# Rewriting windowed attention plus a soft mixture of experts: batch pairs transposed as one 32-bit word, eight units, a list scheduler

## The chip, the cores and the metric

The kernel runs on one core of a Trainium2 chip. The metric is the device time of that core in microseconds (us), the median of the runs. Engines are named as in the profile: PE (TensorE matmuls), PEld (its weight loads), DVE (VectorE), ACT (ScalarE), POOL (GpSimd), SP (SyncE). The clock that the throttle grants to PE has two values in the records here, 1.0 and 0.5, called full and half.

## The reference, cut to what matters

```python
batch, n_heads, seq, head_dim = 8, 8, 576, 64          # q, k, v in fp32
rel = pos[:, None] - pos[None, :]
mask_plain = (rel >= 0) & (rel < 32)                    # heads 0..3
mask_dil   = (rel >= 0) & (rel < 128) & (rel % 4 == 0)  # heads 4..7
attn = softmax(where(mask, q @ k.T / 8, -1e9)) @ v
x = attn, as 4608 tokens x 512
# soft mixture of experts: 8 experts of 4 slots each, D = 512, F = 1024
logits = x @ phi                                        # 4608 x 32
d = softmax(logits, axis=0);  slot_input = d.T @ x
slot_out[e] = relu(slot_input[e] @ w1[e]) @ w2[e]
c = softmax(logits, axis=1);  return c @ slot_out
```

Both softmaxes need the logits of all tokens, and the experts need the slot inputs summed over all tokens. So there is attention over all batches first, then a tail that no attention work can hide: FFN1, FFN2, and the output. The inputs are 61.9 MB and the output 9.4 MB.

## The kernel before

It handles a batch at a time, each batch in two steps (plain heads, dilated heads). Tokens lie on partitions as loaded, 24 tokens to a partition, so PE transposes q, k and v, and ACT copies the result from PSUM (the tiles ps_0 to ps_2, where PE leaves it) back into token order. The dilated heads get their own order (all tokens of one residue modulo 4 together). After that a 96-query block needs only a 128-key window of either kind.

```python
def st_A(g, r):                    # q and k of one step, one residue of the token number
    def pe(t):
        for c1 in range(6):
            for hx in range(2):
                i_ = t.transpose(pbf[64 * hx:64 * hx + 64, 128 * c1:128 * c1 + NR],
                                 src[0:NR, 2 * typ + hx, 4 * c1 + r, :], ident[0:NR, 0:NR])
    pv = pbf[:, 0:768].rearrange("x (c h u) -> x c h u", c=6, h=2)
    def ev(dst, t, off):
        d = dst[:, :, off:off + S]
        if typ == 0:
            d = d.rearrange("x h (p c r) -> x r c h p", c=6, r=4)[:, r]   # plain order
        else:
            d = d.rearrange("x h (r p c) -> x r c h p", r=4, c=6)[:, r]   # dilated order
        return lambda ac: ac.activation(d, pv[:, :, :, PCH * t:PCH * t + NPP], ACTF.Copy)
    op("act", ev(QT[par], 0, 0), r=[pb], **{key: [b_QT[par]]})       # 128 x 288 bf16, scattered
    op("act", ev(KT[par], 1, HALO), r=[pb], **{key: [b_KT[par]]})
...                                # st_V: the same for v, into VT
def st_P(g, half):                 # probabilities times values: 96 weight columns
    i_ = t.matmul(po[0:QB, hx, 65 * m:65 * m + 65],
                  pts[m // 3][0][:, hx, QB * (m % 3):QB * (m % 3) + QB], ...)
def st_X(b, c):                    # x transposed for the logits
    if c >= 2:                     # the dilated heads go back to token order in this copy
        d = d.rearrange("p (s r) -> p r s", r=4)
def st_L(b):                       # logits, and two exps: token order, dilated order
    i_ = t.matmul(lg[:, hf, 0:288], phi_pad[:, c]..., XT[:, c, 288 * hf:288 * hf + 288], ...)
    op("act", ... expT ... ACTF.Exp, accum_out=csum[:, b:b + 1])
    op("act", ... expP[:].rearrange("p (r h s) -> p h s r", r=4, h=2) ... ACTF.Exp)
```

The order of the operations is a fixed loop over 16 steps, written by hand.

The softmax here doesn't subtract the row's maximum and nothing guards it: scores larger than these inputs give would overflow.

## Time and profile before

387.83 us (387.59 and 388.07), two runs. From the page of the profiled run come the busy times, three of the rows of forty slices (each digit is tenths of busy time; PEclk is the granted clock in tenths) and the chain that ended last, by engine and by line:

```profile
PE 230.0 (60%) x3056; PEld 170.5 (44%) x3056; DVE 140.6 (36%) x242; ACT 297.6 (77%) x302; POOL 54.5 (14%) x108
...
ACT  1398999799979997999799978997899764120660
...
PEclk9999999999999999999999999999999999999995
DMA  7999994059005900599055005600660066000599
...
ACT 52%; PE 20%; issue 15%; DVE 7%; DMA 2%; POOL 0%; ACTq 0%
ACT VT L378 17%; ACT KT L352 13%; ACT QT L352 12%; ACT PT L419 8%; PE ps_2 L339 2%; DMA stg<-in_k_dram 2%; PE ps_0 L651 2%; DVE XB L447 2%; DVE w1r L676 2%; PE ps_0 L339 2%; PE ps_2 L394 2%; ACT expP L486 1%; PE ps_0 L459 1%; PE ps_0 L599 1%; PE ps_1 L670 1%
```

ACT is busy nearly all the time and leads the chain; DMA holds 2% of it and idles every other few slices after the first seven. The table of stretches shows it more sharply. A batch takes 38.6 us, and these are two of them (start and end, length, busy time of each engine with the number of instructions, granted clock, DMA share, GB/s landed):

```profile
80.10:118.70 38.60, 25.53 (x359) 20.13 (x357) 14.04 (x25) 35.41 (x37) 5.16 (x10) 1.00 0.40 74
118.70:157.30 38.60, 25.51 (x359) 20.07 (x357) 14.03 (x25) 35.40 (x37) 5.14 (x10) 1.00 0.40 74
```

ACT works 35.4 of 38.6 us. What on? The groups by form (line, engine, operation, output and input by name, shape and type, count, then busy us and mean ns of one, idle time before it):

```profile
L378 ACT ACTIVATE VT<-ps_2 128x288 bf16<-128x288 bf16 x30 | 40.9, 1634 | 0.0
L352 ACT ACTIVATE QT<-ps_0 128x288 bf16<-128x288 bf16 x26 | 33.3, 1281 | 14.3 <-PE ps_0 L339 13.8
L419 ACT ACTIVATE PT<-ps_0 128x576 bf16<-128x576 f32 x32 | 26.2, 820 | 12.8 <-PE ps_0 L413 12.8
L486 ACT ACTIVATE expP<-ps_0 128x576 bf16<-128x576 f32 x4 | 10.3, 2575 | 0.0
```

A copy of 288 elements takes 1.3 to 1.7 us and an exp of 576 elements 0.82 us. The copies differ in that their output is bf16 elements scattered through the row. All nine groups of them sum to 274 us. The second exp of the logits, L486, scatters its output too and takes 2.58 us.

One reading needs care. The clock row shows 9, full speed, from the start. The timeline of PE (start, length, engine and line, count) has the logits of one batch, eight matmuls of 288 columns:

```profile
87.20 2.08 PE L478 MATMUL ps_0<-XT,phi_pad 128*128 128x288 bf16 x8 [0.67 <-ACT PT L419]
```

In the trace their starts lie 240 ns apart inside each half of four, which is 1.2 columns per ns. FFN1's groups of 512 columns start 430 ns apart and drop to 216 ns at 345.6 us, exactly where the first record of a full clock begins. So attention ran at half clock: a slice without a record is drawn as full. Other timed runs of this kernel list mean clocks of 0.60 to 0.91 with the same time (386.6 to 388.8 us), where the profiled one lists 0.988: a listed mean counts all time without a record as full (0.988 is 385.6 us less half of the last 9.3, the only ones recorded at half), so it says little of the time before the first record.

### The profile page before, as it was taken

What the parts mean: (1) busy time and instruction counts of PE and PEld (TensorE: products, weight loads), DVE (VectorE), ACT (ScalarE), POOL (GpSimd) and SP (SyncE); (2) the same over time, 40 slices, a digit from 0 to 9 for tenths busy, and PEclk for the clock granted to TensorE, in tenths of its full rate; (3) what the DMA queues carried; (4) which work ended last, traced back from release to release, by engine and by line L of the source; (5) the groups of instructions that cost most, each with busy time, mean ns of one, the idle gap of its engine ahead of it and who ended that gap; (6) DMA issues with size and microseconds to landing.
All of it is one profiled execution on the core that took longest, in us unless ns stands there. A gap on an engine that the chain in (4) does not pass through costs nothing.

```text
span 385.6 us, 7144 instructions
## 1 busy us (share of the span) xinstructions
PE 230.0 (60%) x3056; PEld 170.5 (44%) x3056; DVE 140.6 (36%) x242; ACT 297.6 (77%) x302; POOL 54.5 (14%) x108
## 2 busy tenths in 40 slices
PE   0223672676467646764676468646864676479750
PEld 0212451565456545654565456445644565245100
DVE  7501332453245324532453245324532473411760
ACT  1398999799979997999799978997899764120660
POOL 6990400050005000600040000000000000000000
PEclk9999999999999999999999999999999999999995
DMA  7999994059005900599055005600660066000599
GB/s 138 217 205 213 218 208 90 3 90 205 2 2 83 205 8 2 85 218 205 8 91 95 2 2 108 111 2 0 110 113 2 0 110 111 0 2 2 210 405 364
DMA packets 12623, 40.89 MB, mean 106 GB/s; under 512 B 3633, under 2 KB 3633, under 8 KB 10545
## 3 DMA queue, kind: packets, MB, share of 16 engines
q0 software_dynamic: 9472, 30.94, 42.7%
q1 hardware_dynamic: 3120, 9.50, 6.3%
q8 instruction: 24, 0.39, 0.4%
q14 instruction: 7, 0.05, 0.0%
HBM read 61.93 MB, written 9.44 MB: 185 GB/s over the span
## 4 chain that ended last, share of the span: by engine, by line
ACT 52%; PE 20%; issue 15%; DVE 7%; DMA 2%; POOL 0%; ACTq 0%
ACT VT L378 17%; ACT KT L352 13%; ACT QT L352 12%; ACT PT L419 8%; PE ps_2 L339 2%; DMA stg<-in_k_dram 2%; PE ps_0 L651 2%; DVE XB L447 2%; DVE w1r L676 2%; PE ps_0 L339 2%; PE ps_2 L394 2%; ACT expP L486 1%; PE ps_0 L459 1%; PE ps_0 L599 1%; PE ps_1 L670 1%
## 5 line engine op out<-in xcount | busy, mean ns | idle before, releaser
L352 ACT ACTIVATE QT<-ps_0 128x288 bf16<-128x288 bf16 x26 | 33.3, 1281 | 14.3 <-PE ps_0 L339 13.8
L422 DVE TENSOR_TENSOR PT<-PT,mask_d 128x576 bf16<-128x576 bf16 x32 | 14.7, 459 | 73.9 <-ACT PT L419 73.8
L378 ACT ACTIVATE VT<-ps_2 128x288 bf16<-128x288 bf16 x30 | 40.9, 1634 | 0.0
L352 ACT ACTIVATE KT<-ps_0 128x288 bf16<-128x288 bf16 x26 | 40.0, 1539 | 0.0
L419 ACT ACTIVATE PT<-ps_0 128x576 bf16<-128x576 f32 x32 | 26.2, 820 | 12.8 <-PE ps_0 L413 12.8
L419 ACT ACTIVATE PT<-ps_1 128x576 bf16<-128x576 f32 x32 | 26.4, 826 | 11.4 <-PE ps_1 L413 11.4
L352 ACT ACTIVATE KT<-ps_2 128x288 bf16<-128x288 bf16 x20 | 33.3, 1667 | 0.0
L469 DVE COPY XT<-ps_0 128x576 bf16<-128x576 bf16 x15 | 14.8, 983 | 47.8 <-PE ps_0 L459 47.8
L339 PE MATMUL ps_0<-ident,stg 112*64 112x112 bf16 x312 | 20.1, 300 | 17.1 <-DMA stg<-in_k_dram 15.1
L232 POOL DMA_DIRECT2D stg<-in_q_dram x16 | 9.5, 597 | 146.0 <-PE ps_0 L339 130.0
L352 ACT ACTIVATE KT<-ps_1 128x288 bf16<-128x288 bf16 x18 | 28.8, 1602 | 0.0
L352 ACT ACTIVATE QT<-ps_2 128x288 bf16<-128x288 bf16 x20 | 27.8, 1388 | 0.7
L422 DVE TENSOR_TENSOR PT<-PT,mask_p 128x576 bf16<-128x576 bf16 x32 | 14.9, 467 | 32.6 <-ACT PT L419 32.6
L394 PE MATMUL ps_2<-ident,VT 128*128 128x128 bf16 x114 | 15.7, 309 | 16.6 <-ACT VT L378 16.6
L378 ACT ACTIVATE VT<-ps_1 128x288 bf16<-128x288 bf16 x18 | 24.1, 1604 | 0.0
L352 ACT ACTIVATE QT<-ps_1 128x288 bf16<-128x288 bf16 x18 | 24.0, 1331 | 0.0
L339 PEld LDWEIGHTS ps_0<-ident,stg 112*64 112x64 bf16 x312 | 14.6, 164 | 20.7 <-issue 17.1
L398 DVE COPY VN<-ps_2 128x768 bf16<-128x768 bf16 x19 | 10.4, 550 | 33.4 <-PE ps_2 L394 33.4
L378 ACT ACTIVATE VT<-ps_0 128x288 bf16<-128x288 bf16 x16 | 21.5, 1614 | 0.0
L469 DVE COPY XT<-ps_1 128x576 bf16<-128x576 bf16 x16 | 15.6, 975 | 13.5 <-PE ps_1 L459 13.5
L262 POOL DMA_DIRECT2D stg<-in_moe_w_dram x6 | 3.2, 538 | 116.5 <-PE ps_0 L339 93.4
L413 PE MATMUL ps_1<-QT,KT 64*128 64x96 bf16 x192 | 13.5, 271 | 10.2 <-ACT KT L352 9.6
(113 smaller groups left out, 531.0 us busy)
## 6 DMA issues: line engine op xcount, KB each, us to landing
out_dram<-w1r SPq DMA_DIRECT2D x18, 512.0 KB, 5.0
w1r<-in_moe_w_dram POOLq DMA_DIRECT2D x8, 1024.0 KB, 14.4
stg<-in_moe_w_dram POOLq DMA_DIRECT2D x6, 1024.0 KB, 8.0
stg<-in_q_dram POOLq DMA_DIRECT2D x16, 288.0 KB, 6.5
stg<-in_k_dram POOLq DMA_DIRECT2D x16, 288.0 KB, 9.5
stg<-in_v_dram POOLq DMA_DIRECT2D x32, 144.0 KB, 9.5
w2r<-in_moe_w_dram POOLq DMA_DIRECT2D x2, 1024.0 KB, 21.2
phi_st<-in_moe_phi_dram SPq DMA_DIRECT2D x1, 64.0 KB, 1.9
```

The lines of the kernel that those rows point to most:

```text
L232: res.append(g.dma_start(stg[p0:p0 + NPP, s, 0:6144].rearrange("p (g x) -> p g x", g=4), src[b, half::2, :, :].rearrange("h (p c) d -> p h ...
L339: i_ = t.transpose(pbf[64 * hx:64 * hx + 64, 128 * c1:128 * c1 + NR], src[0:NR, 2 * typ + hx, 4 * c1 + r, :], ident[0:NR, 0:NR])
L352: return lambda ac: ac.activation(d, pv[:, :, :, PCH * t:PCH * t + NPP], ACTF.Copy)
L378: op("act", lambda ac, d=d, typ=typ: ac.activation(d, pv[:, :, :, PCH * typ:PCH * typ + NPP], ACTF.Copy), r=[pb], **{"w" if r + typ == 0 e ...
L394: i_ = t.transpose(pbf[:, 128 * m:128 * m + 128], VT[:, typ, half, QB * m:QB * m + 128], ident[:, :])
L398: op("dve", lambda vv: vv.tensor_copy(vt[:, half, :, :, 0:64], pbf[:, 0:768].rearrange("p (m x d) -> p m x d", m=NB, x=2)), r=[pb], w=[vb[ ...
L413: i_ = t.matmul(sc[:, hx, QB * mm:QB * mm + QB], KT[par][64 * hx:64 * hx + 64, half, QB * m:QB * m + 128], QT[par][64 * hx:64 * hx + 64, h ...
L419: op("act", lambda ac: ac.activation(pt[:], sc[:, :, 0:3 * QB], ACTF.Exp, scale=SCALE), r=[scb], w=[ptb])
L422: op("dve", lambda vv: vv.tensor_tensor(pt[:], pt[:], mk.unsqueeze(1).to_broadcast([128, 2, 3 * QB]), AluOp.mult), r=[b_mask[typ]], w=[ptb])
L447: op("dve", lambda vv: vv.tensor_tensor(xd, pv[:, :, :, 0:64], rv[:].unsqueeze(3).to_broadcast([QB, 2, NB, 64]), AluOp.mult), r=[pob, rvb] ...
L469: op("dve", lambda vv: vv.tensor_copy(d, i_), r=[pb], **{"w" if c == 0 else "a": [b_XT]})
L651: i_ = t.matmul(sp_[32 * j:32 * j + 32, :], hT[:, hi, cc, j, :], w2v[e][:, cc, :], start=(hi == 0 and cc == 0), stop=(hi == 1 and cc == 7))
```

## The change

The intent: one unit is a pair of batches and one kind of heads, so eight units in all. Loading puts the two batches on neighbouring partitions, so after the transposes their columns are neighbours, and one 32-bit word carries both. ACT then moves 864 words in one instruction, in place of six bf16 copies of 288. These words are also written in runs of 18 or more neighbours (72 tokens to a partition instead of 24), and it is the read from PSUM that now has a step, of 192 bytes. So two things change in the copies, the word and the runs. The source runs of a load become 18 KB. Scores and V transposes read every second column. The operations are no longer in a written order: each has a planned cost, and a list scheduler orders them. It can put filler matmuls into PE's planned idle time, but its window is empty here.

The core of the diff (the whole kernel was rewritten; cuts marked):

```diff
+QB = 96; HALO = 32; NU = 8
+FILL = (9.0, 0.0)                       # window for filler matmuls: empty
...
+for t, src in enumerate((q, k, v)):
+    for bpar in range(2):                # rows of the two batches interleaved
+        rows = src[2 * bp + bpar].rearrange("h (p c) d -> (h p) (c d)", c=CT)[32 * ty:32 * ty + 32]
+        res.append(g.dma_start(stg[32 * t + bpar:32 * t + 32:2, s, :]..., rows...))
...
+i_ = t.transpose(bankb2(pt, a)[64 * hx:64 * hx + 64, 96 * kk:96 * kk + 96],
+                 src[:, hx, c, :], ident[0:96, 0:96])
-        return lambda ac: ac.activation(d, pv[:, :, :, PCH * t:PCH * t + NPP], ACTF.Copy)   # x 192
+            t32 = TT[:, u % 2, :].bitcast(F32)
+            return ac.activation(d, sv, ACTF.Copy)                  # 864 words, x 32
...
-                  pts[m // 3][0][:, hx, QB * (m % 3):QB * (m % 3) + QB],
+                  sbt(pts[i])[:, o_:o_ + 128],                       # 128 weight columns
...
-        if c >= 2:  d = d.rearrange("p (s r) -> p r s", r=4)        # scattered XT copy
+        d, s_ = sbt(xt)[:, x, :], bankb(px)[:, 0:S]                 # plain XT copy
+        rhs = sbt(x1)[:, c - 2, :].rearrange("p (r i) -> p i r", r=4)[:, lo // 4:hi // 4]
-    op("act", ... expP ... ACTF.Exp)                                # second logits exp
...
-i_ = t.matmul(psA[64 * typ:64 * typ + 64, 32 * c:32 * c + 32], x_, et[:, NB * typ + m, :], ...)
+i_ = t.matmul(psA[32 * g:32 * g + 32, 256 * ty:256 * ty + 256], et[:, i, :], xb[:, m, :], ...)
...
-for step in range(-1, 2 * B + 2):  st_B(g, 0); st_S(g, 0, 0); st_A(g + 1, 0); ...
+P.schedule(filler, FILL)
```

## The prediction

> **What bounds the kernel before.** ScalarE. The stretch table gives it 35.6 of every 38.6 us batch; the chain of waits puts 52% of the span on it and only 2% on DMA. The groups by form say why: the copies that put q, k and v back into token order (QT, KT, VT, 128x288 bf16) take 1.28 to 1.67 us each, some 274 us in all, though an exp of twice the elements takes 0.82 us. They write scattered bf16 elements, about 4 ns each. The 40-slice rows show DMA saturated early (205 to 218 GB/s of bf16 landing, twice that read), later mostly waiting. From the slot result to the end takes 27 us.

> **A second reading.** The clock row shows 9, but single matmuls of the logits (288 columns) start 240 ns apart and 128-column transposes 107 ns: 1.2 columns per ns. FFN1 starts at 430 ns per group of 512 columns and drops to 216 ns at 345.6 us, at the first clock record. So attention ran at half clock, and the row shows missing records as full. [...] 3.4 us stretches over 90% busy, mostly with transposes, released nothing.

> **What changes.** Two batches are transposed as neighbouring columns, so one 32-bit word carries both; 32 evictions of 864 words replace 192 scattered ones. At the exp rate (0.65 us per 576 when alone) one is about 0.95 us: 31 us instead of 274. The second logits exp (2.58 us) goes, as do the scattered XT copies (1.44 us, now 0.46). ScalarE falls to 10 to 11 us per unit, VectorE to 12 to 13 us.

> **What binds next.**
> - DMA: 61.9 MB at about 424 GB/s is 146 us, or 13.4 us per unit with one or two weights.
> - TensorE at half clock, from the spacings seen, per unit: input transposes 5.8, scores 1.9, V transposes 2.6, PV 2.7 (128-column weights), X transposes 1.9, logits 1.9, slot weights 1.0, slot sums 0.6: 18.4 us, and about 2 us for tiling-mode changes (0.13 us each in the trace). At full clock about 11.5 us.

> So the clock decides. At full clock DMA binds: loads end near 150 us, then the last FFN2 part and 27 us of output: about 185 us. At half clock: first data at 13 us, eight units of 20 us, a tail of the last softmax, fold, FFN1 and FFN2 of about 25 us, output 27 us: about 230 us. The kernel has code for filler matmuls but its window is empty and over half of its work is transposes. I expect mostly half clock, with released stretches.

> **Prediction: 210 us, range 183 to 234. Faster by over 2%: 0.985; within 2%: 0.008; slower: 0.007.**

> **What would show each step.** Right: ScalarE busy below 120 us; evictions near 0.95 us; TensorE groups leading the chain of waits in the middle, transposes spaced 80 ns per pair (half clock); first clock record late. If instead pairs are near 42 ns apart, the chain's middle should be DMA and the time about 185 us.

> **What would make it wrong.** Evictions that read PSUM with a 192-byte step could take 1.5 us or more; stride-2 operands could slow scores and V transposes; a fixed order planned for other durations could stall engines.

## The result, and the profile after

210.75 us, the median of 209.28 and 212.23, against 387.83 before, on the same chip. The ratio is 0.543, with a 95% interval of 0.539 to 0.547. Ratios here are the mean time of one kernel's runs over that of the other's runs in the same rounds, so not quite the ratio of the quoted medians. Executions over 1.5% slower than the fastest of the same kernel are left out of the means. The output is correct. The profiled run spans 207.6 us.

The same parts of the page as before:

```profile
PE 153.9 (74%) x2840; PEld 110.4 (53%) x2840; DVE 107.8 (52%) x256; ACT 94.0 (45%) x135; POOL 35.8 (17%) x72
...
PE   0058977699988579989597998977897979898000
...
ACT  2015657665546566555476555773110100099200
...
PEclk9999999999999799999969999996555599999955
DMA  6999999999999999999999696089999000069998
...
PE 54%; DVE 23%; ACT 6%; issue 5%; DMA 4%; POOL 1%; DVEq 0%; POOLq 0%
PE ps L514 14%; PE ps L657 10%; DVE PT L564 6%; PE ps L824 5%; PE ps L574 5%; DVE XB L613 5%; PE ps L630 5%; DVE WD L868 4%; DMA stg<-in_v_dram 4%; PE ps L549 4%; DVE VN L579 3%; PE ps L602 3%; ACT PT L556 3%; PE ps L770 3%; PE ps L690 2%
```

ACT fell from 297.6 to 94.0 us and from 52% to 6% of the chain. PE leads the chain now. DMA is busy to slice 22 (about 115 us) and yet has 4% of the chain: its loads are ahead of the work. The three groups that answer to the readings of before, by form:

```profile
L531 ACT ACTIVATE TT<-ps 128x864 f32<-128x864 f32 x32 | 28.3, 895 | 27.0 <-PE ps L514 26.9
L657 PE MATMUL ps<-XT,phi_pad 128*128 128x384 bf16 x32 | 15.0, 600 | 0.0
L657 PE MATMUL ps<-XT,phi_pad 128*128 128x192 bf16 x32 | 8.1, 385 | 1.4 <-DVE XB L613 0.8 <-DVE XT L639 0.6
```

The 32 word copies take 28 us together, where 192 bf16 copies took 274. In the same profile ACT's exps with contiguous output take 651 ns for 576 elements (L663) and 810 for 768 (L556), 0.83 ns for each element more. Drawn on to 864 elements that makes an estimate of 890 ns, and the trace's 895 agrees. The scattered bf16 copies of before don't: the same line drawn back to 288 elements gives an estimate of 412 ns, and they took 1281 to 1667.

PE's clock is read from spacing again, since the first record is at 25.8 us. The timeline of PE, the first and the fifth group of input transposes, and the stall near 68 us:

```profile
12.89 5.97 PE L514 MATMUL ps<-ident,stg 96*64 96x96 bf16 x144 [12.89 <-DMA stg<-in_v_dram]
...
27.14 0.96 PE L514 MATMUL ps<-ident,stg 96*64 96x96 bf16 x36
...
67.65 0.34 PE L574 MATMUL ps<-ident,TT 128*128 128x128 bf16 x3
70.33 0.48 PE L574 MATMUL ps<-ident,TT 128*128 128x128 bf16 x3 [2.33 <-issue]
```

Before 25.8 us, 144 transposes take 5.97 us: a pair every 80 ns, half clock. From 27.14 us, 36 take 0.96 with the last one's own length in it: a pair every 40 to 43 ns, full clock. The records list full clock from 25.8 to 141.9 us but for 70.2 to 73.6 and 104.4 to 107.8, then half from 141.9 to 165.8, then full to 196.5. So most of attention ran at full clock.

The third and fourth lines show a pause of 2.33 us inside one operation of six transposes, with no wait on any other engine. There are three such pauses, 2.0 to 2.6 us from one matmul's start to the next, at 34.6, 67.8 and 101.4 us; the two dips of the clock follow the last two.

Two pairs of units by stretch (the columns as before), and POOL's wait in 47.4 to 115.5 us (who and what, whom it waited for, us in total, times, longest):

```profile
47.40:81.50 34.10, 28.60 (x637) 21.52 (x635) 21.16 (x46) 19.43 (x28) 6.75 (x14) 0.95 1.03 214
81.50:115.50 34.00, 29.18 (x645) 21.90 (x642) 21.56 (x47) 20.09 (x28) 5.15 (x10) 0.95 1.00 209
```

```profile
POOL stg L396 <- PE ps L514: 38.1, 3, 16.0
```

A pair of units takes 34 us, 17.0 per unit: PE is busy 28.6 to 29.2 of it at a mean clock of 0.95, and the DMA share is 1.00 to 1.03 (209 to 214 GB/s landing). POOL, which issues the loads, waits 38 us of that stretch for PE to free the buffers. So the loads run without a gap, three buffers ahead, and PE uses them at about the same pace. Which of the two sets the pace can't be read off this; an experiment has to tell.

### The profile page after: what moved, and what is told of

Its sections match the earlier page's. It is cut to its first block, busy times and chain, and to the rows that moved or that the text cites. A ratio compares the mean times of both kernels' runs of the same rounds, so it can differ in the third digit from the quotient of the medians.

```text
span 207.6 us, 6274 instructions
## 1 busy us (share of the span) xinstructions
PE 153.9 (74%) x2840; PEld 110.4 (53%) x2840; DVE 107.8 (52%) x256; ACT 94.0 (45%) x135; POOL 35.8 (17%) x72
## 4 chain that ended last, share of the span: by engine, by line
PE 54%; DVE 23%; ACT 6%; issue 5%; DMA 4%; POOL 1%; DVEq 0%; POOLq 0%
PE ps L514 14%; PE ps L657 10%; DVE PT L564 6%; PE ps L824 5%; PE ps L574 5%; DVE XB L613 5%; PE ps L630 5%; DVE WD L868 4%; DMA stg<-in_v_dram 4%; PE ps L549 4%; DVE VN L579 3%; PE ps L602 3%; ACT PT L556 3%; PE ps L770 3%; PE ps L690 2%
## 5 line engine op out<-in xcount | busy, mean ns | idle before, releaser
L556 ACT ACTIVATE PT<-ps 128x768 bf16<-128x768 f32 x48 | 37.6, 810 | 15.4 <-PE ps L549 15.4
L514 PE MATMUL ps<-ident,stg 96*64 96x96 bf16 x1152 | 32.4, 216 | 14.6 <-DMA stg<-in_v_dram 12.9
L531 ACT ACTIVATE TT<-ps 128x864 f32<-128x864 f32 x32 | 28.3, 895 | 27.0 <-PE ps L514 26.9
L514 PEld LDWEIGHTS ps<-ident,stg 96*64 96x64 bf16 x1152 | 28.7, 117 | 16.7 <-DMA stg<-in_v_dram 12.9
L613 DVE TENSOR_TENSOR XB<-ps,RV 96x768 bf16<-96x768 f32 x32 | 30.2, 945 | 0.5
L579 DVE COPY VN<-ps 128x768 bf16<-128x768 bf16 x32 | 17.4, 544 | 20.0 <-PE ps L574 20.0
L657 PE MATMUL ps<-XT,phi_pad 128*128 128x192 bf16 (+1 forms) x64 | 21.7, 492 | 1.4 <-DVE XB L613 0.8
L549 PE MATMUL ps<-TT 64*128 64x96 bf16 x384 | 17.2, 221 | 7.2 <-ACT PT L556 2.7
L602 PE MATMUL ps<-VN,PT 128*128 128x65 bf16 x384 | 18.5, 198 | 2.9 <-DVE VN L579 1.1
L574 PE MATMUL ps<-ident,TT 128*128 128x128 bf16 x192 | 18.2, 244 | 2.8 <-issue 2.3
L602 PEld LDWEIGHTS ps<-VN,PT 128*128 128x128 bf16 x384 | 14.8, 100 | 5.3 <-DVE VN L579 1.5
L574 PEld LDWEIGHTS ps<-ident,TT 128*128 128x128 bf16 x192 | 13.1, 110 | 8.0 <-issue 5.1
L639 DVE COPY XT<-ps 128x576 bf16<-128x576 bf16 x17 | 7.7, 455 | 16.5 <-PE ps L630 16.4
L630 PEld LDWEIGHTS ps<-ident,XB 96*128 96x128 bf16 x192 | 10.9, 106 | 9.0 <-issue 6.2
L564 DVE TENSOR_TENSOR PT<-PT,mask_p 128x768 bf16<-128x768 bf16 x24 | 12.9, 543 | 1.2 <-ACT PT L556 1.2
L663 ACT ACTIVATE expT<-ps 128x576 bf16<-128x576 f32 x8 | 5.2, 651 | 18.1 <-PE ps L657 18.1
```

What stands on the lines that cost most here:

```text
L514: i_ = t.transpose(bankb2(pt, a)[64 * hx:64 * hx + 64, 96 * kk:96 * kk + 96], src[:, hx, c, :], ident[0:96, 0:96])
L531: return ac.activation(d, sv, ACTF.Copy)
L549: i_ = t.matmul(pair(sc)[:, hx, QB * x:QB * x + QB], win(u, 1, h01, blk_, bpar)[64 * hx:64 * hx + 64], win(u, 0, h01, blk_, bpar)[64 * hx: ...
L556: op("act", lambda ac: ac.activation(sbt(pt)[:, 0:768].rearrange("p (x n) -> p x n", x=2), pair(sc)[:, :, 0:384], ACTF.Exp, scale=SCALE), ...
L564: return dv.tensor_tensor(p_, p_, m.unsqueeze(1).to_broadcast([128, 2, 384]), AluOp.mult)
L574: i_ = t.transpose(bankb(pv)[:, 128 * m:128 * m + 128], win(u, 2, h01, m, bpar), ident[:, :])
```

## The experiments

Twelve kernels ran. The kernel before took 387.4 to 387.9 us, so times are compared as they are; the changed kernel itself has only the two runs above. Times are medians.

### 1. The logits read contiguous columns

The copy of the dilated heads' transposed x goes back to token order, and the logits read it without a step.

```diff
+            if ty:
+                d = d.rearrange("p (s r) -> p s r", r=4)
+                s_ = s_.rearrange("p (r s) -> p s r", r=4)
...
-                        rhs = sbt(x1)[:, c - 2, :].rearrange("p (r i) -> p i r", r=4)[
-                            :, lo // 4:hi // 4]
+                        rhs = sbt(x1)[:, c - 2, lo:hi]
```

> Edit: the copy that evicts a transposed X of the dilated heads reads PSUM with a step and writes the natural token order, so the logits matmuls read contiguous columns; the result stays right and every engine keeps its order. Theory A (TensorE's own order of work is the bound, and the 288-byte step of the moving operand is what makes 384 columns take 632 ns instead of 162): the group of 8 logits matmuls falls from 2.45 us to about 1.1 us, on the chain in all 8 batches, so the time falls by 9 to 12 us to about 199 to 202 us. Rival B (DMA, which the page shows saturated until 115 us, is the bound): only the last two batches matter and the time falls by less than 4 us. A copy that reads PSUM with a step should cost 0.65 us on ScalarE as before and up to 0.75 us on VectorE (0.46 before).

Measured: correct, 199.66 us (198.61 to 199.87), ratio to before 0.5146 (0.513 to 0.516), inside what theory A said. Groups of the logits and of the copy, by form:

```profile
L659 PE MATMUL ps<-XT,phi_pad 128*128 128x384 bf16 x32 | 6.5, 326 | 0.0
L659 PE MATMUL ps<-XT,phi_pad 128*128 128x192 bf16 x32 | 4.0, 248 | 2.3 <-DVE XT L642 1.3 <-ACT XT L643 1.0
...
L642 DVE COPY XT<-ps 128x576 bf16<-128x576 bf16 x17 | 10.0, 595 | 9.8 <-PE ps L630 9.7
```

The logits' busy time falls from 23.1 to 10.5 us and the whole time by 11.1 us. In the trace, 192 strided columns took 308 to 324 ns and 384 took 632; now 82 and 162. The copy on DVE grew from 455 to 595 ns, on ACT not at all (649). The strided columns cost about 1.65 ns each at full clock, and at half clock hardly more (up to 338 and 656 ns), where contiguous ones take twice as long (160 and 320 ns). So the time of a strided column hardly went with the clock, and that of a contiguous one did. The change had moved this scatter from a copy on DVE to a read on PE, where it was on the chain of waits.

### 2. A sixth of the loads

From the fourth unit on, five of six loads of a unit are left out. The result is wrong.

```diff
-            for t, src in enumerate((q, k, v)):
-                for bpar in range(2):
+            for t, src in enumerate((q, k, v) if u < 3 else (q,)):
+                for bpar in range(2 if u < 3 else 1):
```

> Edit: units 3 to 7 load one sixth of their bytes (q of one batch, the rest is the old unit's data: wrong result on purpose), everything else and the order of every compute engine unchanged; 14.8 MB of the 61.9 MB read are gone. Theory A (TensorE-bound): the distance of two batch pairs stays near 34 us and the time stays within 2% of 210.75 us, because the loads were only prefetch that ran ahead. Rival B (DMA-bound while its row shows 9): the distance falls to about 25 us and the time by more than 15 us.

Measured: 202.87 us (201.24 to 206.9), ratio 0.5213 (0.519 to 0.524). The stretches of the same two pairs of units:

```profile
47.40:78.00 30.60, 27.80 (x644) 20.79 (x640) 21.65 (x47) 19.80 (x28) 2.14 (x4) 1.00 0.48 91
78.00:108.80 30.80, 27.91 (x646) 20.89 (x640) 21.62 (x47) 19.76 (x28) 2.68 (x5) 1.00 0.75 147
```

Neither theory has this size. With DMA at half to three quarters of its load, a pair still takes 30.7 us. So PE's own order sets most of the 34, and the loads 3.4 us of it. Where do the 3.4 us lie? The pauses at 68 and 101 us are gone, each of which idled PE for 2.3 to 2.4 us, and so are the two dips of the clock that followed them. The only pause left is at 34.5 us (1.88 us), while DMA was still full; a dip follows it here, from 36.3 to 39.7 us. The trace shows a 16 KB packet of the instruction queue, about 1 us long, that starts within 0.5 us of the start of each pause (34.16, 67.95 and 101.57 us in the profile after), and the pauses are 1272 PE instructions apart. Most such packets come with no pause. So the coincidence with full DMA is shown, and the cause of the pauses is not.

### 3. PE filled with matmuls

The window of the filler matmuls (512 columns, whole array) is opened.

```diff
-FILL = (9.0, 0.0)
+FILL = (9.0, 1000.0)
```

> Edit: the filler window opened from 9 us to the end, nothing else: the planner puts 512-column matmuls of the identity into gaps of TensorE over 0.4 us. Theory A (half clock costs time where it reigns: before 25.8 us, two dips of 3.4 us, 141.9 to 165.8 us): the clock records show full clock nearly throughout, the first four input transposes take 3.4 us instead of 6.0, the last logits 2.45 instead of 3.05, FFN1 3.6 instead of 5; the time falls by 5 to 9 us to about 202 to 206 us. Rival B (fillers stand in TensorE's queue before work that comes earlier than planned, and cost what they win): 209 us or more.

Measured: correct, 213.71 us (212.78 to 215.92), ratio 0.5522 (0.549 to 0.556); 1.7% slower than the change without fillers (ratio 0.543). Its first fillers and input transposes on PE:

```profile
10.88 8.81 PE L882 MATMUL ps<-mask_p,ident 128*128 128x512 bf16 x29 [10.88 <-DVE mask_d L465]
19.62 2.57 PE L514 MATMUL ps<-ident,stg 96*64 96x96 bf16 x112
```

The clock was released at 15.7 us instead of 25.8, and the tail ran at full clock. But the planner took 216 ns for each filler; those before 15.7 us ran at half clock, and they put the start of the first transposes off from 12.9 to 19.6 us. The first logits came at 54.9 us instead of 46.7. Fillers planned for idle time land, in a fixed order, ahead of work that is ready. The gain in clock did not pay for it, as rival B said. Nor was the clock full nearly throughout, as theory A had it: between its release and 115 us it was at half for 23.9 us (39.6 to 46.5, 56.7 to 70.3 and 111.3 to 114.7), against 6.8 us from 25.8 us on without fillers.

### 4. The old kernel with contiguous copies

In the kernel before, the 192 copies write runs of neighbouring bf16 elements. All else stays. The result is wrong.

```diff
-            if typ == 0:
-                d = d.rearrange("x h (p c r) -> x r c h p", c=6, r=4)[:, r]
-            else:
-                d = d.rearrange("x h (r p c) -> x r c h p", r=4, c=6)[:, r]
+            d = dst[:, :, off:off + S].rearrange("x h (r c p) -> x r c h p", r=4, c=6)[:, r]
```

> Edit to the kernel before: the 192 copies of q, k and v write the same number of elements to contiguous runs of 24 (wrong result on purpose); nothing else. Theory A (a copy costs about 4 ns per scattered bf16 element because of where it writes): the copies fall from 1.28 to 1.67 us to about 0.45 us, ScalarE falls below TensorE, and a batch takes about 26 us at half clock instead of 38.6: about 285 us in all, 270 to 300. Rival B (the cost is the PSUM read or the shape of the instruction): copies stay over 1 us and the time over 370 us.

Measured: 280.48 us (271.13 to 283.73; the runs of this kernel differ with the clock), as theory A said. Two groups by form, and the busy times:

```profile
L348 ACT ACTIVATE KT<-ps 128x288 bf16<-128x288 bf16 x64 | 27.1, 424 | 0.0
L370 ACT ACTIVATE VT<-ps 128x288 bf16<-128x288 bf16 x64 | 20.4, 436 | 6.8 <-PE ps L363 6.8
...
PE 204.4 (74%) x3055; PEld 156.6 (57%) x3056; DVE 141.3 (51%) x242; ACT 139.7 (51%) x302; POOL 54.9 (20%) x108
```

The same copies take 419 to 436 ns, near the estimate of 412. So the scatter of 2-byte elements, and nothing else in the copy, cost the 0.9 to 1.2 us. About 107 of the 177 us that the change gained come with this alone. PE is then the busiest engine at 74%, mostly at half clock; which parts of the rewrite brought the rest is not taken apart here.

### 5. FFN2 in another order, with the contiguous logits

FFN2's 128 matmuls no longer run eight in a row on one group of 32 array columns; four experts take turns, each on its own group.

```diff
-                    for cc in range(lo, hi_):
-                        i_ = t.matmul(pair(sp_)[32 * j:32 * j + 32, h_, 0:256], hT[:, hi, cc, j, :], ...)
+                for cc in range(8):
+                    for j in range(4):
+                        i_ = t.matmul(pair(sp_)[32 * j:32 * j + 32, h_, 0:256], hT[:, hi, cc, j, :], ...)
```

> Edit: e_logits, and FFN2 issues its 128 matmuls in turn over the four column groups instead of 8 in a row in one group; result right, order of everything else unchanged. Theory: 8 matmuls in a row in one column group start 109 ns apart because they run one after another; in turn over four groups they should run four at a time, so FFN2 falls from 11.2 us to about 4 us, all of it between the last slot sums and the output: about 192 us (199.66 for e_logits alone). Rival: FFN2 waits for the last weights to land, and the time stays over 197 us.

Measured: correct, 195.36 us (189.58 to 198.24). FFN2 in the kernel of experiment 1, then in this one (groups by form):

```profile
L826 PE MATMUL ps<-stg,hT 128*32 128x256 bf16 x80 | 7.2, 273 | 0.5 <-DVE hT L799 0.5
L826 PE MATMUL ps<-TT,hT 128*32 128x256 bf16 x48 | 4.6, 273 | 0.0
```

```profile
L826 PE MATMUL ps<-stg,hT 128*32 128x256 bf16 x80 | 3.7, 273 | 0.5 <-DVE hT L799 0.5
L826 PE MATMUL ps<-TT,hT 128*32 128x256 bf16 x48 | 1.9, 273 | 0.0
```

FFN2 as a whole went from 11.2 us (169.2 to 180.4 in the profile after) to 3.7 us. In the timeline the matmuls of four column groups start within 0.01 us of each other (158.84 us) and the next four 0.11 us later, where matmuls in a row on one group started 109 ns apart one by one: so the groups stream at once. The theory's 4 us for FFN2 are shown. In the time the median falls by 4.3 us, less than the 7.5 us saved in FFN2, and lies between the theory's 192 us and the rival's 197; the gain in time has no firm size. The four runs were 189.58 us at a mean clock of 0.925, 194.14 at 0.885, 196.58 at 0.884 and 198.24 at 0.851: the spread goes with the clock in the main.

### 6. Fillers in the tail only

Experiment 5 with the filler window opened from 140 us on (planned time).

```diff
-FILL = (9.0, 0.0)
+FILL = (140.0, 1000.0)
```

> Edit: e_logits_ffn2 and the filler window opened only for the last part of the plan (from 140 us of the plan's own time, 12 groups of 1 to 6 fillers). Theory A (the tail runs at half clock[...], and that costs FFN1 1.5 us and the last softmax 2 us): the clock stays full through FFN1 and the time is 2 to 4 us below e_logits_ffn2. Rival B (fillers cost what they win, as in e_fill): the same or more.

Measured: correct, 194.98 us (191.1 to 197.02). The clock stayed full from 107.0 to 178.6 us, through the tail. (In the profile after, without fillers, it fell at 141.9 us; PE streamed 0.34 of the 3.4 us before that.) The time does not differ from experiment 5 by more than either one's spread, so whether the fuller clock in the tail pays is not settled.

### 7. Fewer changes of tiling mode

Experiment 5 with a scheduler that prefers work in the mode that PE is in: 66 changes of mode instead of 128.

```diff
-                t0, o, got = min((x for x in c if x[0] <= lim), key=lambda x: (x[1].key, x[1].id))
+                t0, o, got = min((x for x in c if x[0] <= lim), key=lambda x: (
+                    x[1].key + 2.0 * (e == "pe" and x[1].mode != mode), x[1].id))
```

> Edit: e_logits_ffn2 with a planner that prefers, for TensorE, work in the tiling mode of the work before it (66 changes between row-tiled, column-tiled and whole-array groups in the program instead of 128). Theory A (each change costs about 0.11 us of TensorE's own time and TensorE is the bound): 62 changes fewer save about 7 us: about 185 us. Rival B (a worse order makes TensorE wait for its inputs, or the changes are hidden): within 2 us of e_logits_ffn2, or slower.

Measured: correct, 202.58 us (200.35 to 203.84), ratio 0.5205 (0.517 to 0.524); slower than experiment 5. In the profile after, at full clock, a matmul that comes after a change of mode starts some 0.1 us later than one that doesn't: from a score to a V transpose the starts lie 133 to 135 ns apart and back 151 to 152, from a V transpose to an X transpose, without a change, 55 to 56. That makes an estimate of about 6 us for 62 changes. Rival B holds: the saving was lost, and PE ran at half clock more often, with a mean of 0.839 in the profiled run (0.851 to 0.925 in the runs of experiment 5). From the first release to 145 us it was at half clock for 30.7 us, against 9.0 in the profile of experiment 5, and PE's busy time is 139.4 us against 129.7: that is most of the 12.7 us between the two profiled runs. Which of the moved operations costs the time was not traced.

### 8. 96 weight columns for probabilities times values

As in the kernel before, in place of 128.

```diff
-sbt(pts[i])[:, o_:o_ + 128],
+sbt(pts[i])[:, o_:o_ + QB],
```

> Edit: the changed kernel with 96 stationary columns in PV as in the kernel before, instead of 128 (32 of them unused); result right, order unchanged. Theory: [...] with 96 the spacing of PV's matmuls rises from 34 ns to 60 to 80 ns, 48 of them per unit on TensorE's chain: 1.3 to 2.2 us per unit, 10 to 17 us in all, about 221 to 228 us. Rival: the loads are hidden behind the matmuls and the time stays within 2% of 210.75 us.

Measured: correct, 222.81 us (219.26 to 226.47), ratio 0.5696 (0.565 to 0.575): 12 us slower. The row of the granted clock and the groups by form of the matmuls and their weight loads, then the weight loads of the profile after:

```profile
PEclk9999999999998555555555999999555579999955
...
L602 PE MATMUL ps<-VN,PT 128*96 128x65 bf16 x384 | 27.5, 232 | 1.5 <-ACT PT L556 0.7 <-DVE VN L579 0.4 <-DVE PT L564 0.3
L602 PEld LDWEIGHTS ps<-VN,PT 128*96 128x96 bf16 x384 | 24.5, 149 | 3.8 <-ACT PT L556 1.1 <-DVE VN L579 0.6 <-DVE PT L564 0.4
```

```profile
L602 PEld LDWEIGHTS ps<-VN,PT 128*128 128x128 bf16 x384 | 14.8, 100 | 5.3 <-DVE VN L579 1.5 <-ACT PT L556 1.0 <-DVE PT L564 0.7
```

A load of 128 weight columns takes 100 ns in the mean and one of 96 takes 149. The two runs differ in clock (0.899 and 0.805), but the profile after has the same contrast in itself (154 ns for the loads of 96 columns at L690), and so has the kernel before at half clock (192 ns for 96 columns at L438, 118 and 119 for the 128 of the scores). The matmuls start 33 ns apart at full clock with 128 weight columns and 45 ns with 96 (45 at L690 of the profile after, too). That is 384 times 12 ns, about 5 us. The 60 to 80 ns that the theory expected come at half clock only (80 ns with 96 columns, 55 with 128), so its time came out right with the step too large. The rest goes with the clock, half from 70.2 to 121.4 us in the profiled run.

### 9 to 11. What releases the clock

The prediction expected mostly half clock of a kernel with over half of its work in transposes. Three kernels vary experiment 3's fillers: four 128-column transposes; then one 512-column matmul on a quarter of the array; then pairs of transposes in the form of the kernel's own input transposes.

```diff
-                i_ = te.matmul(bank(t)[:, 0:512], ident[:, :], mask[0]...[:, 0:512], ...)
+                for k_ in range(4):                                            # 9
+                    i_ = te.transpose(bankb(t)[:, 128 * k_:128 * k_ + 128], mask[0]..., ident[:, :])
...
+                i_ = te.matmul(bank(t)[0:64, 0:512], ident[0:64, 0:64],        # 10
+                               mask[0]...[0:64, 0:512], ...)
...
+                for k_ in range(5):                                            # 11
+                    for hx in range(2):
+                        i_ = te.transpose(bankb(t)[64 * hx:64 * hx + 64, 96 * k_:96 * k_ + 96],
+                                          mask[0]...[0:96, 64 * hx:64 * hx + 64], ident[0:96, 0:96])
```

> The fillers of the run with filler matmuls, with each 512-column matmul replaced by four 128-column transposes: the same columns, the same plan, the same waits. Theory A (transposes do not count as activity for the clock[...]): the clock is not released near 15.7 us, as it was with filler matmuls that began about 11 us, but only with the first dense stretch of scores, logits and slot sums, at 25 us or later. Rival B (transposes count as well as matmuls): first release between 14 and 18 us. The time itself tells little, 205 to 222 us either way, since the fillers cost TensorE the same time.

> The run with transposes as fillers released the clock at 14.0 us, so transposes do count. Yet this kernel's own input transposes, dense from 13 to 18.4 us, did not release it before 25.8 us. They differ from the fillers in using a part of the array: 96 rows by 64 columns each, two side by side. Here each filler is one 512-column matmul, dense in time, but on 64 rows by 64 columns: a quarter of the array. Theory A (the clock counts how much of the array works): no release before 22 us. Rival B (it counts only whether something streams): release between 14 and 18 us, as with the other fillers.

> Fillers in the form of the kernel's own input transposes: pairs of 96 rows by 64 columns, 96 columns long, dense in time from about 11 us. Theory A (share of the array, here three quarters while a pair runs): no release before 22 us if three quarters is too little. Rival B (streaming alone counts): release between 14 and 18 us. If the quarter-array run is not released and this one is, then three quarters suffices, and the input transposes of the unfilled kernel released nothing for want of a long enough dense stretch (5.4 us with gaps).

Measured: all three correct; 217.44 us (two runs), 226.6 and 244.03 us (one run each, state unknown). The times don't matter here, the clock's first release does. The first groups on PE of the three kernels, in that order:

```profile
10.83 8.14 PE L883 MATMUL ps<-ident,mask_p 128*128 128x128 bf16 x116 [10.83 <-DVE mask_d L465]
```

```profile
10.84 12.58 PE L882 MATMUL ps<-mask_p,ident 64*64 64x512 bf16 x29 [10.84 <-DVE mask_d L465]
23.35 5.59 PE L514 MATMUL ps<-ident,stg 96*64 96x96 bf16 x144
28.87 1.91 PE L882 MATMUL ps<-mask_p,ident 64*64 64x512 bf16 x8
```

```profile
10.82 6.85 PE L884 MATMUL ps<-ident,mask_p 96*64 96x96 bf16 x223 [10.82 <-DVE mask_d L465]
```

- Transposes on the whole array: first full-clock record at 14.0 us, 3.2 us after they begin. Rival B holds: transposes count. (The 512-column matmuls of experiment 3 released it at 15.7 us, 4.8 us after they began; the stretches of the measure below begin at another time in each run.)
- Matmuls on a quarter of the array: 29 in 12.58 us, 427 ns apart, streaming without a gap at half clock for 12.5 us, and no release. The release came at 28.4 us, after 5 us of input transposes. The eight fillers after it take 1.91 us, 1/4 of the array and full clock. Theory A holds: the share of the array counts.
- Pairs of transposes on three quarters: release at 14.9 us. So three quarters is enough when dense.

The kernel's own 144 input transposes show the same without any filler. In the profiled run of experiment 5, where they run from 12.9 to 17.8 us, they released the clock at 16.5 us; in the profile after the same transposes, from 12.9 to 18.9 us, did not. What differs is where the stretches of the measure below begin: in experiment 5 the transposes fill the one from 13.1 to 16.5 us (share 0.75), in the profile after they fill neither of two (0.59 and 0.67).

### 12. Nine fillers at the start

If 3.4 us of the whole array release the clock, nine fillers before the first transposes are enough. This is experiment 5 with just those.

```diff
-FILL = (9.0, 0.0)
+FILL = (9.0, 10.3)
...
-                n = min(int((gap - 0.15) / 0.216), 64)
+                n = min(int((gap - 0.15) / 0.216), 9)
```

> The version with contiguous logits and reordered FFN2, plus only nine filler matmuls of the whole array before the first input transposes. If the clock is released by the share of the array that streams within 3.4 us, nine fillers at half clock (about 3.9 us from 10.9 us) followed by dense transposes on three quarters of the array release it between 14 and 18.5 us in every run, where the version without them was released at 16.5 us in its profiled run and, by its clock of 0.85 to 0.885, later in others. The fillers delay the first transposes by about 2 us. Theory A (the early release pays): median 189 to 194 us, against 195.4 without. Rival B (the early phase waits for loads anyway, so only the delay remains): 195 to 199 us.

Measured: correct, 192.98 us (190.35 to 194.92, six runs), ratio 0.4954 (0.493 to 0.498). PE at the start, then in the profiled run of experiment 5, which has no fillers:

```profile
10.79 4.02 PE L884 MATMUL ps<-mask_p,ident 128*128 128x512 bf16 x9 [10.79 <-DVE mask_d L465]
14.73 3.50 PE L514 MATMUL ps<-ident,stg 96*64 96x96 bf16 x144
```

```profile
12.89 4.92 PE L514 MATMUL ps<-ident,stg 96*64 96x96 bf16 x144 [12.89 <-DMA stg<-in_v_dram]
```

With the fillers the clock was released at 15.3 us, and the 144 transposes took 3.50 us instead of 5.97 in the profile after. They end at 18.2 us against 18.9 there, though they began 1.8 us later. But in experiment 5, the base of this one, the clock was released at 16.5 us and they ended at 17.8: against that profile the fillers gained nothing at the start. The median is the best of all the kernels here, inside what theory A expected. The gain over experiment 5 (2.4 us) is less than that kernel's spread. So a gain in time is not shown. The early release is shown in the one profiled run; that all runs have it, and that those of experiment 5 were "later in others", can't be read from their mean clocks.

## Why the prediction was right or wrong

The time was right: 210 us predicted, range 183 to 234, 210.75 measured. Part of that is luck, since two errors of opposite sign met.

- **"What bounds the kernel before. ScalarE."** Right, and experiment 4 shows it: with contiguous copies alone the old kernel takes 280 us.
- **"At the exp rate ... one is about 0.95 us: 31 us instead of 274."** Right: 895 ns, 28.3 us. ScalarE's whole busy time is 94.0 us, below the 120 named. The worry about reading PSUM with a step did not come true.
- **"I expect mostly half clock."** Wrong. In the profiled run the clock was full for all but 6.8 of the 116 us from 25.8 to 141.9. The failed step is the premise that is cut from the second reading, and with it the reading of the trace of before that "3.4 us stretches over 90% busy ... released nothing". Busy is not streaming: in the kernel before, the stretch from 198.8 us has PE busy throughout and a streaming share of 0.67. There, the array's streaming share in 3.41 us of attention never exceeds 0.69, and the one stretch that reaches 0.81, in FFN1, released the clock. The dense new order reaches 0.86 in the stretch before 25.8 us. Experiment 9 shows that transposes release the clock, and 10 that the share of the array matters. When it was released was partly luck: the input transposes did it in experiment 5 and not in the profile after.
- **"At full clock about 11.5 us" per unit, with DMA then binding at 13.4.** Mis-sized: a unit took 17.0 us. Within the pair from 67.4 to 101.4 us, PE's groups fill 21.7 us, or 10.9 per unit, where half of the 18.4 us in the estimate is 9.2. The other 12.2 us, 6.1 per unit, are the 45 gaps between groups, from the start of a group's last matmul to the start of the next group: one pause of 2.55 us, changes of mode, and waits for ACT and DVE. The estimate had 2 us per unit for all of these. Strided logits (the 12.6 us of busy time that experiment 1 removed over 8 batches) were named as a worry for scores and V transposes and not for the logits, where they were; the 4-byte step of the scores shows next to no cost (mostly a pair of 96 columns every 43 to 44 ns at full clock, where those of the input transposes take 40 to 43).
- **"If instead pairs are near 42 ns apart, the chain's middle should be DMA and the time about 185 us."** Wrong. Pairs were 40 to 43 ns apart, the chain was PE, and the time 210. Experiment 2 shows the loads to be worth 3.4 us per pair of units, not the difference to 13.4 us per unit.
- **"First data at 13 us", "output 27 us".** Right: 12.9 us, and 26 us.
- **"A tail ... of about 25 us."** Mis-sized: from the last probabilities times values (143 us) to the output (181 us) it took 38. The last logits and slot sums ran at half clock up to 158 us, and FFN2 took 11.2 us since it ran on one column group at a time; in another order it takes 3.7.

The number, 210, lay between the prediction's two cases, 185 us at full clock and 230 at half. Neither came: the clock was mostly full, and 17.0 us per unit with a tail of 38 put that case some 25 us above its 185. The first error made the prediction too high and the others too low.

Left open: what the 2.0 to 2.6 us pauses of PE are; which part of the rewrite, beyond the contiguous copies, brought how much; whether early or late fillers gain time beyond the spread; and why stretches of like share, 0.70 to 0.76, sometimes release the clock and sometimes not.

## What to carry to other kernels

When a copy is slow, compare its time per element with a contiguous one of the same engine: scattered 2-byte writes cost three to four times as much here (1281 to 1667 ns for 288 elements, 419 to 436 contiguous). Writing runs of neighbours removed that in experiment 4, still with 2-byte elements; pairing two batches into one 32-bit word halves the elements besides. A scatter that is dropped from a copy can come back as a strided read, so look at which engine then reads it and whether that engine leads the chain: here ACT's stepped read of PSUM cost nothing (895 ns against the estimate of 890), and PE's of the logits 12.6 us. Read PE's clock from the spacing of like matmuls, and judge whether it will be released by how much of the array streams over a few us (0.70 or more of it, in 58 of the 62 releases here), not by PE's busy time.
